# A state-space layer and a feed-forward layer, forward and backward, on one core: factored convolution transforms, smaller feed-forward chunks, and parameter gradients made where their operands are

## The chip, the cores and the metric

One core of one Trainium2 chip. The metric is the time on the device of one execution, in microseconds. Most executions of a kernel agree within 0.3%. One run of the kernel before, at 4296 us in one of the series, was slow and is in no ratio.

In the profile's lines PE is the matmul engine and PEld its loads of stationary operands; DVE (vector), ACT (activations) and POOL (GpSimd) do the elementwise work; SP issues transfers (DMA). Matmuls leave their sums in banks of PSUM (tiles named ps), and to evict a sum is to copy it out with DVE or ACT.

## The reference, cut to what matters

```
xn  = layernorm(x)                                  # x: 2048 x 576, bf16
K   = Re( sum_n C * exp(dt*A*l) * dt*B )            # S4 kernel: 576 channels, 128 states, 2048 lags
y   = irfft(rfft(pad(xn)) * rfft(pad(K))) + xn*Dskip
ffn = (relu(xn @ W_gate) * (xn @ W_up)) @ W_down    # 576 -> 4608 -> 576
out = x + y + ffn
# returned: out and, for the given grad_out, the gradients of x, A, B, C (re, im), log_dt, Dskip, W_gate, W_up, W_down
```

Two independent parts (S4 and FFN) share a core. FFN is mostly matmul. S4 is mostly vector work: 128 x 2048 complex exponentials for each of 576 channels, and the reductions of their gradients, between four rounds of Fourier transforms.

## The kernel before: the parts that matter

Two Python generators give out FFN and S4 work in small units. S4 gets 0.8 units of estimated time for each of FFN's. When FFN has run out, the rest of S4 runs alone, and then the final tiles, which add the two parts' results and finish the gradient of x.

```
# pacing
while True:
    r = next(fgen, None)
    if r is None: break
    ffn_t += float(r)
    while not s4_done and s4_t < ratio * (ffn_t - lead):     # ratio = 0.8, lead = 40
        c = next(sgen, None)
        ...
for _ in sgen: pass
final_main(...)

# kernel rows (gen_kgen): Y is made, used for K, and also stored for the gradients
nc.vector.tensor_tensor(Yr[:], E[:], c_[:], op=ALU.mult)
nc.vector.tensor_tensor(Yi[:], E[:], s_[:], op=ALU.mult)
...
nc.sync.dma_start(y_dram[0, :, ...], Yr[:]);  nc.sync.dma_start(y_dram[1, :, ...], Yi[:])

# transforms (gen_fwd): dense 1024-column DFT matrices, KC = 4 accumulated matmuls a tile (8 and more in the inverse)
for kc in range(KC):
    nc.tensor.matmul(ps[:, :DH], lhsT=Fmat[:, kc, mc*P:(mc+1)*P], rhs=sig[:, kc, hf*DH:(hf+1)*DH], ...)

# end of the S4 gradients (gen_grads), five times
ft = ctx.enter_context(tc.tile_pool(name="g_ft", bufs=2))
...
ob = ft.tile([P, N], BF16, name="g_ob")
nc.scalar.activation(ob[:dsz], src[:dsz], ACT.Copy, scale=dtk)
nc.sync.dma_start(outs[name][d0:d0 + dsz, :], ob[:dsz])                     # six of these
...
nc.sync.dma_start(outs["log_dt"][d0:d0+dsz].rearrange("(p o) -> p o", o=1), dldb[:dsz])  # 128 values, one a partition
```

Of the kernel before, what the change touches and what calls it, by code (L numbers as in the profile page):

```python
# [9 lines left out]
BF16 = mybir.dt.bfloat16  # L10
# [7 lines left out]
Q = 128  # L18
# [3 lines left out]
CFG = dict(mode="interleave", ratio=0.8, lead=40.0, ffn_prio="none")  # L22
STATE = dict(phase="none")


def dchunks(D):
    return [(k, k * P, min(P, D - k * P)) for k in range((D + P - 1) // P)]


def padded(D):  # L30
    return ((D + P - 1) // P) * P


def make_consts(nc, consts, NA):
    C = {}
    C["ident_bf"] = consts.tile([P, P], BF16, name="ident_bf")
    make_identity(nc, C["ident_bf"][:])
    C["ident_f"] = consts.tile([P, P], F32, name="ident_f")
    make_identity(nc, C["ident_f"][:])
    for name, val in (("mcol", MAGIC), ("hpcol", math.pi / 2), ("nhpcol", -math.pi / 2)):  # L40
        C[name] = consts.tile([P, 1], F32, name=name)
        nc.vector.memset(C[name][:], val)
    C["bvals"] = consts.tile([P, Q], F32, name="bvals")
    nc.gpsimd.iota(C["bvals"][:], pattern=[[1, Q]], base=0, channel_multiplier=0, allow_small_or_imprecise_dtypes=True)
    C["lvals"] = consts.tile([P, NA], F32, name="lvals")
    C["qavals"] = consts.tile([P, NA], F32, name="qavals")
    nc.gpsimd.iota(C["qavals"][:], pattern=[[Q, NA]], base=0, channel_multiplier=0, allow_small_or_imprecise_dtypes=True)
    nc.gpsimd.iota(C["lvals"][:], pattern=[[P, NA]], base=0, channel_multiplier=1, allow_small_or_imprecise_dtypes=True)
    pcol = consts.tile([P, 1], F32, name="pcol")
    nc.gpsimd.iota(pcol[:], pattern=[[0, 1]], base=0, channel_multiplier=1, allow_small_or_imprecise_dtypes=True)  # L50
    half = consts.tile([P, 1], F32, name="halfp")
    nc.vector.tensor_scalar(half[:], pcol[:], 0.5, -0.25, op0=ALU.mult, op1=ALU.add)
    nc.vector.tensor_scalar(half[:], half[:], MAGIC, None, op0=ALU.add)
    nc.vector.tensor_scalar(half[:], half[:], MAGIC, None, op0=ALU.subtract)
    par = consts.tile([P, 1], F32, name="par")
    nc.vector.scalar_tensor_tensor(par[:], half[:], -2.0, pcol[:], op0=ALU.mult, op1=ALU.add)
    C["sgn"] = consts.tile([P, 1], F32, name="sgn")
    nc.vector.tensor_scalar(C["sgn"][:], par[:], -2.0, 1.0, op0=ALU.mult, op1=ALU.add)
    C["nsgn"] = consts.tile([P, 1], F32, name="nsgn")
    nc.vector.tensor_scalar(C["nsgn"][:], par[:], 2.0, -1.0, op0=ALU.mult, op1=ALU.add)  # L60
    return C


def transpose_blocks(nc, psum_t, src, nblk, ident_bf):
    pt = psum_t.tile([P, 8, P], BF16, name="pt")
    for k in range(nblk):
        nc.tensor.transpose(out=pt[:, k, :], in_=src[:, k * P:(k + 1) * P], identity=ident_bf[:])
    return pt


def ln_forward(tc, nc, ctx, x_ap, g_ap, L, D, xn_dram, rinv_all, xnT_dram, gT_dram, psum_t, ident_bf):
    ST = L // P
    DP = padded(D); NDK = DP // P
    big = ctx.enter_context(tc.tile_pool(name="ln_big", bufs=1))
    sb = ctx.enter_context(tc.tile_pool(name="ln_sb", bufs=3))
    tb = ctx.enter_context(tc.tile_pool(name="ln_tb", bufs=2))
    small = ctx.enter_context(tc.tile_pool(name="ln_small", bufs=1))
    nsub = 2 if D > nc.vector.BN_STATS_FMAX else 1
    assert D % nsub == 0
    fsz = D // nsub  # L80
    x_all = big.tile([P, ST, D], BF16, name="x_all")
    nc.sync.dma_start(x_all[:], x_ap.rearrange("(t p) d -> p t d", p=P))
    mv_all = small.tile([P, ST, nc.vector.BN_AGGR_DIM], F32, name="mv_all")
    for st in range(ST):
        stats = sb.tile([P, nsub, nc.vector.BN_STATS_DIM], F32, name="stats")
        for s in range(nsub):
            nc.vector.bn_stats(out=stats[:, s, :], in_=x_all[:, st, s * fsz:(s + 1) * fsz])
        nc.vector.bn_aggr(out=mv_all[:, st, :], in_=stats[:])
    mvb = small.tile([P, ST, 2], BF16, name="mvb")
    nc.vector.tensor_copy(mvb[:], mv_all[:])  # L90
    mvf = small.tile([P, ST, 2], F32, name="mvf")
    nc.vector.tensor_copy(mvf[:], mvb[:])
    veb = small.tile([P, ST], BF16, name="veb")
    nc.vector.tensor_scalar(veb[:], mvf[:, :, 1], 1e-5, None, op0=ALU.add)
    sdb = small.tile([P, ST], BF16, name="sdb")
    nc.scalar.activation(sdb[:], veb[:], ACT.Sqrt)
    sdf = small.tile([P, ST], F32, name="sdf")
    nc.vector.tensor_copy(sdf[:], sdb[:])
    nc.vector.reciprocal(rinv_all[:], sdf[:])
    GRP = 4 if ST % 4 == 0 else 1  # L100
    for st0 in range(0, ST, GRP):
        xT_st = tb.tile([P, NDK, GRP * P], BF16, name="xT_st")
        gT_st = tb.tile([P, NDK, GRP * P], BF16, name="gT_st")
        for j in range(GRP):
            st = st0 + j
            xc = sb.tile([P, D], BF16, name="xc")
            nc.vector.tensor_scalar(xc[:], x_all[:, st, :], mvf[:, st, 0:1], None, op0=ALU.subtract)
            xn = sb.tile([P, DP], BF16, name="xn")
            if DP > D:
                nc.gpsimd.memset(xn[:, D:DP], 0.0)  # L110
            nc.vector.tensor_scalar(xn[:, 0:D], xc[:], rinv_all[:, st:st + 1], None, op0=ALU.mult)
            nc.sync.dma_start(xn_dram[st * P:(st + 1) * P, :], xn[:, 0:D])
            pt = transpose_blocks(nc, psum_t, xn, NDK, ident_bf)
            nc.scalar.copy(xT_st[:, :, j * P:(j + 1) * P], pt[:, 0:NDK, :])
            gt = sb.tile([P, DP], BF16, name="gt")
            if DP > D:
                nc.gpsimd.memset(gt[:, D:DP], 0.0)
            nc.gpsimd.dma_start(gt[:, 0:D], g_ap[st * P:(st + 1) * P, :])
            pt2 = transpose_blocks(nc, psum_t, gt, NDK, ident_bf)
            nc.vector.tensor_copy(gT_st[:, :, j * P:(j + 1) * P], pt2[:, 0:NDK, :])  # L120
        nc.sync.dma_start(xnT_dram[:, :, st0 * P:(st0 + GRP) * P], xT_st[:])
        nc.gpsimd.dma_start(gT_dram[:, :, st0 * P:(st0 + GRP) * P], gT_st[:])


def load_dn(nc, pool, ap, D, N, name, eng):
    DK = dchunks(D); NDK = len(DK)
    t = pool.tile([P, NDK, N], BF16, name=name)
    nfull = sum(1 for (_, _, dsz) in DK if dsz == P)
    if nfull > 0:
        eng.dma_start(t[:, 0:nfull, :], ap[0:nfull * P, :].rearrange("(k p) n -> p k n", p=P))  # L130
    for (k, d0, dsz) in DK:
        if dsz < P:
            eng.dma_start(t[:dsz, k, :], ap[d0:d0 + dsz, :])
    return t


def load_dt(nc, pool, log_dt, D, name):
    DK = dchunks(D); NDK = len(DK)
    ldt = pool.tile([P, NDK], BF16, name=name + "_l")
    nc.vector.memset(ldt[:], 0.0)  # L140
    for (k, d0, dsz) in DK:
        nc.sync.dma_start(ldt[:dsz, k:k + 1], log_dt[d0:d0 + dsz].rearrange("(p o) -> p o", o=1))
    dt = pool.tile([P, NDK], F32, name=name)
    nc.scalar.activation(dt[:], ldt[:], ACT.Exp)
    return dt


def s4_params(tc, nc, ctx, D, N, aps, ident_f, psum_s4, T_dram):
    assert N == P
    DK = dchunks(D)  # L150
    pool = ctx.enter_context(tc.tile_pool(name="s4p", bufs=1))
    tmp = ctx.enter_context(tc.tile_pool(name="s4p_tmp", bufs=2))
    raw = {name: load_dn(nc, pool, aps[name], D, N, f"raw_{name}", nc.sync) for name in ("A_re", "A_im", "B_re", "B_im", "C_re", "C_im")}
    dt = load_dt(nc, pool, aps["log_dt"], D, "dt")
    dt2pi = pool.tile([P, len(DK)], F32, name="dt2pi")
    nc.vector.tensor_scalar(dt2pi[:], dt[:], 1.0 / TWO_PI, None, op0=ALU.mult)
    for (k, d0, dsz) in DK:
        ar = tmp.tile([P, N], F32, name="ar")
        nc.vector.tensor_scalar(ar[:dsz], raw["A_re"][:dsz, k, :], dt[:dsz, k:k + 1], None, op0=ALU.mult)
# [20 lines left out]
def gen_kgen(tc, nc, ctx, L, D, N, T_dram, xp_dram, y_dram, k_dram, C, psum_s4, SC=32, DG=8):  # L180
# [12 lines left out]
    mcol, hpcol, bvals = C["mcol"], C["hpcol"], C["bvals"]  # L193
    qav = C["qavals"]
    k_view = k_dram[:].rearrange("(a p) d -> p a d", p=P)
    LAG = 1
    pending = []
    kst_done = []
    kst_count = {}
# [864 lines left out]
```

## Time and profile before

| before | value |
|---|---|
| time, median of 5 | 2557.6 us (2547.6 to 2564.5) |
| mean granted clock | 0.90 |
| PE at its streaming rate (worked out in the prediction: 1869; from the trace's matmuls: 1858) | 73% of the span |

The page's engine shares, its slices (each digit a fortieth of the span, in tenths) and its chain by engine:

```profile
PE 2048.3 (80%) x15768; PEld 1270.0 (50%) x15768; DVE 1762.9 (69%) x4152; ACT 1427.4 (56%) x2431; POOL 508.0 (20%) x782
...
PE   3899999887997999995499998989998999755400
...
DVE  6798999998999532222999998981220228899944
ACT  2789898988988755531253353354372345445421
...
PEclk8899999998998999998699999999999999756655
...
PE 26%; DVE 21%; issue 17%; ACT 16%; DMA 15%; POOL 3%; SPq 1%; POOLq 0%; ACTq 0%; DVEq 0%
```

Read the slices as columns. PE is at 9 where DVE is at 2 (the transforms). PE's last six digits fall from 7 to 0 while DVE is at 8 and 9, and at 4 in the last two. The chain is spread over everything, a fourth of it PE. Nothing is saturated from end to end.

### The profile page before, as it was taken

The numbers are of one execution on the slowest core, as the hardware profiler recorded it, in microseconds if no ns is written. First come the engines' busy times: TensorE is split into PE (matmuls) and PEld (weight loads), VectorE is DVE, ScalarE is ACT, GpSimd is POOL, SyncE is SP. The second block draws the span as 40 slices with busy tenths as digits, with TensorE's granted clock in tenths as the row PEclk, the third lists the DMA queues.
The fourth block names the chain that finished last, engine by engine and source line by source line (L and its number), as shares of the span: only waits on it lengthen the run. The fifth ranks groups of instructions, "written<-read, shape, count | busy, mean of one in ns | idle before, by whom it ended". The sixth has DMA issues, their size and how long they took to land.

```text
span 2555.4 us, 43178 instructions
## 1 busy us (share of the span) xinstructions
PE 2048.3 (80%) x15768; PEld 1270.0 (50%) x15768; DVE 1762.9 (69%) x4152; ACT 1427.4 (56%) x2431; POOL 508.0 (20%) x782
## 2 busy tenths in 40 slices
PE   3899999887997999995499998989998999755400
PEld 2464554554465466652254454455565665555300
DVE  6798999998999532222999998981220228899944
ACT  2789898988988755531253353354372345445421
POOL 2111121111022111110142233132011112222310
PEclk8899999998998999998699999999999999756655
DMA  7446558556666655466266657457445658776563
GB/s 223 143 143 196 139 127 210 143 126 152 175 146 150 168 139 143 136 176 161 63 162 154 165 114 189 114 114 168 97 105 162 169 148 220 220 215 193 158 146 90
DMA packets 481526, 393.59 MB, mean 154 GB/s; under 512 B 271232, under 2 KB 430496, under 8 KB 478240
## 3 DMA queue, kind: packets, MB, share of 16 engines
q1 hardware_dynamic: 424288, 287.60, 39.9%
q0 software_dynamic: 57024, 103.23, 19.4%
q8 instruction: 123, 2.02, 0.3%
q14 instruction: 91, 0.75, 0.1%
HBM read 229.46 MB, written 161.25 MB: 153 GB/s over the span
## 4 chain that ended last, share of the span: by engine, by line
PE 26%; DVE 21%; issue 17%; ACT 16%; DMA 15%; POOL 3%; SPq 1%; POOLq 0%; ACTq 0%; DVEq 0%
PE ps_s L351 4%; DMA out_dram<-g_ob 3%; PE ps_s L449 3%; PE ps_mm L754 3%; PE ps_mm L752 3%; PE pt L771 2%; PE ps_mm L750 2%; ACT y_E L240 2%; PE ps_mm L785 2%; PE ps_mm L780 2%; PE ps_mm L787 2%; ACT y_c L272 1%; ACT y_s L269 1%; DMA f_gtt<-gT_dram 1%; DMA ffn_acc<-so 1%
## 5 line engine op out<-in xcount | busy, mean ns | idle before, releaser
L762 DVE SCALAR_TENSOR_TENSOR upm<-ps_mm,upb 128x512 bf16<-128x512 f32 x144 | 98.5, 684 | 289.0 <-ACT upb L758 289.0
L820 PE MATMUL ps_mm<-dgN,xs 128*128 128x512 bf16 x720 | 270.3, 383 | 14.2 <-ACT dWdT_sb L822 7.1
L821 PE MATMUL ps_mm<-duN,xs 128*128 128x512 bf16 x720 | 268.6, 383 | 3.4 <-ACT dWdT_sb L822 2.0
L819 PE MATMUL ps_mm<-hN,gs 128*128 128x512 bf16 x720 | 257.8, 382 | 8.9 <-DMA gs<-in_grad_out_dram 8.9
L752 PE MATMUL ps_mm<-xT,wu 128*128 128x512 bf16 x720 | 205.6, 393 | 37.2 <-ACT upb L758 37.2
L796 POOL DMA_DIRECT2D ffn_acc<-so x128 | 118.2, 923 | 492.0 <-ACT so L781 419.3
L750 PE MATMUL ps_mm<-xT,wg 128*128 128x512 bf16 x720 | 201.9, 384 | 8.7 <-DMA wg<-in_B_W_gate_dram 8.7
L785 PE MATMUL ps_mm<-wgT,dgT 128*128 128x288 bf16 x1152 | 196.6, 286 | 8.3 <-ACT so L781 4.5
L754 PE MATMUL ps_mm<-gTt,wdT 128*128 128x512 bf16 x720 | 199.6, 394 | 0.0
L787 PE MATMUL ps_mm<-wuT,duT 128*128 128x288 bf16 x1152 | 190.9, 286 | 0.0
L780 PE MATMUL ps_mm<-wd,hT 128*128 128x288 bf16 x1152 | 175.4, 287 | 9.7 <-ACT so L781 8.4
L781 ACT CAST so<-ps_mm 128x288 bf16<-128x288 f32 x288 | 109.1, 404 | 98.9 <-PE ps_mm L780 47.2
L797 POOL DMA_DIRECT2D dxf_acc<-sx x128 | 116.9, 914 | 106.9 <-DVE sx L791 72.5
L780 PEld LDWEIGHTS <-hT 128*128 128x128 bf16 x1152 | 111.4, 98 | 44.6 <-issue 12.0
L476 PE MATMUL ps_s<-ident_bf,YA 128*128 128x128 bf16 x1152 | 117.9, 275 | 19.4 <-DMA YA<-y_dram 9.6
L785 PEld LDWEIGHTS <-dgT 128*128 128x128 bf16 x1152 | 111.9, 98 | 37.5 <-issue 10.4
L822 ACT CAST dWdT_sb<-ps_mm 128x512 bf16<-128x512 f32 x45 | 26.3, 585 | 181.8 <-PE ps_mm L819 181.8
L787 PEld LDWEIGHTS <-duT 128*128 128x128 bf16 x1152 | 112.1, 98 | 27.4
L476 PEld LDWEIGHTS <-YA 128*128 128x128 bf16 x1152 | 102.5, 127 | 34.5 <-issue 16.1
L820 PEld LDWEIGHTS <-xs 128*128 128x128 bf16 x720 | 70.5, 98 | 97.0 <-issue 11.7
L449 PE MATMUL ps_s<-Wl,Gmat 128*128 128x288 bf16 x768 | 111.7, 290 | 8.5 <-ACT dK_sb L669 3.8
L791 DVE CAST sx<-ps_mm 128x288 bf16<-128x288 f32 x176 | 78.1, 451 | 55.9 <-PE ps_mm L787 45.7
(336 smaller groups left out, 4980.7 us busy)
## 6 DMA issues: line engine op xcount, KB each, us to landing
YA<-y_dram SPq DMA_DIRECT2D x72, 512.0 KB, 4.3
xT<-xnT_dram SPq DMA_DIRECT2D x36, 640.0 KB, 4.6
gTt<-gT_dram SPq DMA_DIRECT2D x36, 640.0 KB, 6.2
ffn_acc<-so POOLq DMA_DIRECT2D x144, 144.0 KB, 4.0
dxf_acc<-sx POOLq DMA_DIRECT2D x144, 144.0 KB, 3.8
gs<-in_grad_out_dram SPq DMA_DIRECT2D x72, 256.0 KB, 3.5
xs<-xn_dram SPq DMA_DIRECT2D x72, 256.0 KB, 3.8
y_dram<-y_Yi SPq DMA_DIRECT2D x72, 256.0 KB, 2.8
```

The lines of the kernel that those rows point to most:

```text
L449: nc.tensor.matmul(ps[:, :DH], lhsT=lt, rhs=rh, start=(i == 0), stop=(i == len(mms) - 1))
L476: nc.tensor.transpose(out=psb[:, dl * N:(dl + 1) * N], in_=ya[:, h0 + dl, :], identity=C["ident_bf"][:])
L750: nc.tensor.matmul(ps_g[:, :SGW], lhsT=wg[:, k, ft * P:(ft + 1) * P], rhs=xT[:, k, :], start=(k == 0), stop=(k == NDK - 1))
L752: nc.tensor.matmul(ps_u[:, :SGW], lhsT=wu[:, k, ft * P:(ft + 1) * P], rhs=xT[:, k, :], start=(k == 0), stop=(k == NDK - 1))
L754: nc.tensor.matmul(ps_h[:, :SGW], lhsT=wdT[:, k, ft * P:(ft + 1) * P], rhs=gTt[:, k, :], start=(k == 0), stop=(k == NDK - 1))
L780: nc.tensor.matmul(ps_o[:, :DH], lhsT=hT[:, ft, j * P:(j + 1) * P], rhs=wd[:, ft, hf * DH:(hf + 1) * DH], start=(ft == 0), stop=(ft == FTC ...
L785: nc.tensor.matmul(ps_x[:, :DH], lhsT=dgT[:, ft, j * P:(j + 1) * P], rhs=wgT[:, ft, hf * DH:(hf + 1) * DH], start=(ft == 0), stop=False)
L787: nc.tensor.matmul(ps_x[:, :DH], lhsT=duT[:, ft, j * P:(j + 1) * P], rhs=wuT[:, ft, hf * DH:(hf + 1) * DH], start=False, stop=(ft == FTC - 1))
L796: nc.gpsimd.dma_start(ffn_acc[st * P:(st + 1) * P, :], so[:], accum_op=ALU.add)
L819: nc.tensor.matmul(ps_d[:, :Fc], lhsT=gs[:, sl, :], rhs=hN[:, st, :], start=(st == 0), stop=(st == ST - 1))
L820: nc.tensor.matmul(ps_g[:, :Fc], lhsT=xs[:, sl, :], rhs=dgN[:, st, :], start=(st == 0), stop=(st == ST - 1))
L821: nc.tensor.matmul(ps_u[:, :Fc], lhsT=xs[:, sl, :], rhs=duN[:, st, :], start=(st == 0), stop=(st == ST - 1))
```

## The change

The mathematics stays and nearly every line is new. Its intent: less PE work, none of S4 left over when FFN ends, and vector work spread evenly. At its core (cuts marked):

```
-    nc.tensor.matmul(... lhsT=Fmat[:, kc, ...] ...)            # x4 a tile, dense 1024-column matrices
+    # 2048 = 128 x 16: 128-point factor, 16-point factor, product, and back
+    nc.tensor.matmul(ps[:, :DH], lhsT=self.S1[:, n2, ri, :], rhs=halves(n2, hf), start=True, stop=True)
+    nc.tensor.matmul(ps[:, :DH], lhsT=CC[:], rhs=src[:, o, hs], ...); nc.tensor.matmul(ps[:, :DH], lhsT=sm[:], ...)
...
-    nc.sync.dma_start(y_dram[0, ...], Yr[:])                   # reloaded in a gradient phase of its own
+    self.group(pend.pop(0), ytp, gp)                           # K and the gradient products from Y while it is there
...
-Fc=512  (9 chunks), xT single-buffered
+Fc = 384 (12 chunks), xT, gT, gq, xs double-buffered; output tiles put between the gate tiles
...
+class Balance:                                                 # each eviction goes to the less loaded of DVE and ACT
+    def copy(self, out, in_, cols, scale=None, fp32=True): ...
...
-while not s4_done and s4_t < ratio * (ffn_t - lead):           # ratio = 0.8
+while s4_open and stt < PACE * (ft - start):                   # PACE = 0.86
...
+    for i in range(4):                                         # final tiles within the last weight gradients
+        self.dw_down(c, i)
+        for t in range(i * 2, i * 2 + 2): final(t)
...
-    nc.sync.dma_start(outs["log_dt"][...].rearrange("(p o) -> p o", o=1), dldb[:dsz])
+    nc.sync.dma_start(self.outs["log_dt"][...].rearrange("(o p) -> o p", o=1), dldb[0:1, 0:dsz])   # one row
```

Down weights have one buffer, `self.wd`. In program order `load_w(c)`, which fills it for chunk c, stands before the four last output tiles of chunk c-1:

```
self.load_w(c)                               # overwrites wd
for j in range(JS):
    self.outdx(c - 1, NSG - 1, j)            # reads wd: now the next chunk's
```

## The prediction

> **What bounds the kernel now.** I read the page's engine shares and its 40 slices first, then busy time per stage (stretches cut where the program changes phase), then the chain of waits in the last 150 us, then the groups by shape, for durations. No engine is busy all the time: PE 80%, DVE 69%, ACT 56%. The stretches show why.
>
> ```profile
> core 0: us, PE busy (x) PEld busy (x) DVE busy (x) ACT busy (x) POOL busy (x), PEclk, DMA share, GB/s
> 0.00:72.00 72.00, 21.63 (x172) 16.46 (x172) 41.81 (x162) 16.53 (x30) 19.87 (x67) 0.80 0.76 233
> ...
> 128.00:768.00 640.00, 577.39 (x4538) 341.39 (x4537) 595.20 (x995) 570.03 (x793) 110.79 (x140) 0.96 0.61 155
> 896.00:1152.00 256.00, 248.21 (x1731) 155.33 (x1729) 68.72 (x178) 127.90 (x287) 35.31 (x47) 0.99 0.56 150
> 1152.00:1216.00 64.00, 32.32 (x160) 14.53 (x159) 17.26 (x67) 7.00 (x12) 7.33 (x14) 0.80 0.66 158
> 1216.00:1728.00 512.00, 437.65 (x2875) 253.32 (x2875) 476.11 (x1186) 220.28 (x445) 147.18 (x223) 0.94 0.56 135
> 1728.00:2048.00 320.00, 297.71 (x2079) 191.41 (x2077) 52.46 (x120) 134.22 (x231) 52.87 (x76) 0.98 0.56 139
> ...
> 2206.00:2410.00 204.00, 116.30 (x1616) 104.02 (x1615) 203.87 (x670) 101.71 (x191) 50.58 (x85) 0.62 0.69 203
> 2410.00:2555.00 145.00, 8.16 (x20) 3.22 (x20) 71.81 (x262) 34.33 (x88) 22.26 (x39) 0.50 0.49 117
> ```
>
> The columns after the engines are granted clock, DMA share and GB/s. The feed-forward part (FFN) runs beside the state-space part (S4), whose phases follow one another. Making the convolution kernel (128 to 768) loads DVE to 93% and ACT to 89%. The forward transforms (896 to 1152) and the inverse ones (1728 to 2048) are PE's, with DVE at 27% and 16%. The products (1216 to 1728) are DVE's, at 93%, with ACT at 43%. At 1152 the Dskip gradient waits for single-buffered loads and PE falls to half. From 2206 FFN has run out: 204 us of parameter gradients bound by DVE, then 145 us in which nearly nothing runs. In the first 72 us there is only layer norm. So the imbalance in time is the bound, more than any engine's total.
>
> The chain inside the last 145 us:
>
> ```profile
> by line: DMA out_dram<-g_ob 60.6%; issue 4.2%; ACT g_ob L551 3.3%; DMA hN<-dxf_acc 3.2%; DMA Rk<-r_dram 2.5%; DMA out_dram<-hN 2.4%; PE ps_s L544 2.3%; ACT hN L876 1.0%; ACT gd_dcr L546 0.9%; ACT L144 0.9%; ACT hN L884 0.8%; SPq L872 0.6%;
> ```
>
> 61% of that stretch is the landing of small gradient tiles whose buffer is wanted again: pure latency.
>
> How densely PE can stream is read from starts in the timeline, because the ends overlap:
>
> ```profile
> 2012.68 1.03 PE L752 MATMUL ps_mm<-xT,wu 128*128 128x512 bf16 x4
> 2013.54 1.24 PE L754 MATMUL ps_mm<-gTt,wdT 128*128 128x512 bf16 x5
> 2014.62 0.78 PE L780 MATMUL ps_mm<-wd,hT 128*128 128x288 bf16 x5
> ...
> 2018.58 1.14 PE L780 MATMUL ps_mm<-wd,hT 128*128 128x288 bf16 x8
> 2019.56 0.65 PE L785 MATMUL ps_mm<-wgT,dgT 128*128 128x288 bf16 x4
> ```
>
> Five of 512 columns take 2014.62 - 2013.54 = 1.08 us, 0.216 each; eight of 288 take 0.98 us, 0.1225 each.
>
> **What the Trainium skill says.** "TensorE: Matmul & The Clock Gate", section "Wait — 56ns, not 53.3ns?": a warm start-to-start is N/2.4 GHz plus about 2.5 ns, with a floor near 25 ns. The trace agrees (0.216 and 0.1225 us), so I estimate 62.5 ns for 144 columns, 162.5 for 384, 55.5 for 128, 29 for 64 and 26 for 16 and 32. The same page, "Part 1: The HAM clock gate", says an idle PE drops to half clock: the tail's 0.62 and 0.50 agree. "ScalarE: Activation LUTs", "What ACT_TABLE_LOAD costs", gives 1283 ns a load; the trace has exactly that, and 100 loads in its six main rows. "VectorE: DVE Perf Modes", "The perf-mode tier table", says two-tensor ops run double rate in bf16 and single in fp32 or from PSUM; agreed, 422 ns against 683 at 512 columns.
>
> ```profile
> L764 DVE TENSOR_TENSOR dgT<-dhb,upm 128x512 bf16<-128x512 bf16 x144 | 60.8, 422 | 28.4 <-ACT dhb L760 26.3
> L254 DVE TENSOR_TENSOR x_Xr<-x_e,x_c 128x512 bf16<-128x512 f32 x18 | 12.3, 683 | 0.1
> L240 ACT ACT_TABLE_LOAD x33 | 42.3, 1283 | 0.6
> L781 ACT CAST so<-ps_mm 128x288 bf16<-128x288 f32 x288 | 109.1, 404 | 98.9 <-PE ps_mm L780 47.2
> ```
>
> **The change, part by part.** It is a rewrite of the same mathematics, so I count instructions of the built programs and price them from the rows.
>
> PE before: 4320 x 0.216 = 933; 5344 of 288 (3456 FFN, 1888 transforms) x 0.1225 = 655; some 3760 transposes x 0.0555 = 209; 2304 small x 0.026 = 60; fp32 and rest 12: about 1869 us at full clock, 73% of the span. PE after: FFN up and gate 2160 x 0.216 = 467; output side 3456 x 0.1225 = 423; weight gradients, no longer padded to 640 rows, 2304 x 0.0625 + 1536 x 0.1625 + 1152 x 0.029 = 144 + 250 + 33; 3616 transposes = 201; the convolution as 128- and 16-point factors instead of dense 1024-column matrices, 1152 x 0.1225 = 141; small 60, rest 12: about 1731. PE saves 138 us.
>
> DVE after, raw row sums: FFN masks and products 144 x (684 + 427 + 422 + 416) = 281; evictions 436, 201; kernel rows Y 144 x (683 x 3 + 421 + 2 x 422) = 477; gradient products and reductions 576 x about 420 = 243; X 155; spectral products, now one pass per frequency, 122; base and final tiles 129; norm, twiddles, parameters 121: about 1730. Neighbours overlap by about 0.08 us (an operation of 1.22 us starts 1.13 before the next), some 250 us over 3570 instructions: about 1480 net against 1763. ACT after: 902 + 192 evictions of 288 x 0.404 to 0.410 = 443; 505 bf16 copies 310; other evictions 320; FFN Relu and copy 172; sines and exponentials 365; 40 table loads instead of over 100, 51: about 1660, net some 1480 against 1427. It takes evictions from DVE by a running balance.
>
> Twelve column chunks of 384 replace nine of 512: 192 more output evictions of 288 and more reloads, the price of room for double-buffered inputs.
>
> Schedule: layer norm by groups of four tiles, so PE starts FFN at about 25 us, not 72. S4 is paced by 0.86 of FFN's estimated time; in PE's order its last matmul stands at about 37 fortieths of the work, so the 350 us tail goes. Parameter gradients are made next to their kernel rows (no reload of 36.9 MB, no separate phase), and final tiles sit within the last weight-gradient matmuls.
>
> Sum by stage. Head 25; FFN before S4, 90 of PE at 0.85, 106. Transforms first half 210 at 0.9, 233. Kernel and gradients: PE 1089; vector work 1510 (S4) + 819 (FFN beside it) raw, less some 283 overlap, over two engines 1023 each. The stage 128 to 768 of before kept PE streaming at about 0.84 with DVE 0.93 and ACT 0.89, so PE at 0.87 to 0.89 looks reachable at 0.83: 1240. Second half of the transforms 266 at 0.9, 296. FFN alone 110 at 0.92, 120. Behind it some 40 us, where the final tiles (16 x 4.2 us of DVE) outlast 37 us of matmul. Together 2060; with a little for waits at the joints, 2070.
>
> **Rivals.** First, three engines near 85% in order may stall each other. For it: the kernel's output side now fills a PSUM bank in 0.37 or 0.73 us, before 0.49 or 0.98, and must be evicted through the same four banks, while ACT runs 1.0 to 1.3 us operations; S4 has two banks. At 0.78 of streaming it is 1731 / 0.78 + 60 = 2280 us. Against it: in the old stage with both vector engines near 90%, PE still streamed 0.84. Second, vector work bounds the middle: if strided evictions cost as the old Kst copy did (771 ns for 128 elements; 144 x 0.5 = 72 us more) and half of the overlap, 150 us, is not had, each vector engine has 1023 + 111 = 1134 there, and at 0.87 that is 1300 instead of 1240: 2130. Third, the mixing works better, PE at 0.91 throughout: 1731 / 0.91 + 60 = 1960. Fourth, transfers: acc reads and writes grow with twelve chunks, but Y no longer goes through memory, so I estimate 360 MB against 394; hidden.
>
> **Range and chances.** 2070 us, 1960 to 2190 for 8 in 10. A gain of 2% needs under 2506; the tail alone is 350 us, so even with the first rival it holds: faster 0.96, same 0.02, slower 0.02.
>
> **What would show it.** Right: granted clock above 0.94 until the last slices; PE's first FFN matmul before 35 us; DVE near 1480 and ACT near 1480 busy, both even over the span; DVE share in the transforms well over the old 16 to 27%; under 80 us after the last output matmul. Wrong: waits of PE for evictions (ps_mm, ps_s released by ACT or DVE) of several hundred us; a middle where PE streams under 0.8; S4 still running after FFN.

## The result, and the profile after

The order of the load of `wd` shown above is a defect of the changed kernel, not of the kernel before. The changed kernel, with which the defect came, took **2112.0 us** (2103.6 to 2115.1, 8 runs) against 2558.8 (2547.6 to 2568.0, 15 runs): ratio **0.825**, 95% interval 0.8233 to 0.8267. Ratios here are the mean time of one kernel's fast runs over the mean of the other's in the same rounds, so not quite the ratio of the quoted medians.

The same parts of the page, after:

```profile
PE 1914.3 (91%) x17726; PEld 1314.0 (62%) x17726; DVE 1527.7 (72%) x3550; ACT 1456.4 (69%) x3070; POOL 227.9 (11%) x292
...
PE   7989999879899999999899999899899899978796
...
DVE  8544665499877898759989599886885375646594
ACT  5655664489778889659889589877786456732563
...
PEclk9999999989999999999999999999999999989899
...
PE 43%; ACT 18%; DMA 11%; DVE 9%; issue 8%; SPq 0%; POOL 0%; ACTq 0%; DVEq 0%; POOLq 0%
```

No digit of PE is below 6, the granted clock never leaves 8 to 9, and PE's share of the chain went from 26 to 43%. By stage (columns: stretch, length, then busy time and instructions of PE, its weight loads, DVE, ACT, POOL; then clock, DMA share, GB/s). The rows are transforms up to the first kernel row; kernel rows and parameter gradients; the other transforms; FFN alone; and the time behind FFN's last output matmul:

```profile
100.00:424.00 324.00, 292.70 (x2305) 192.43 (x2305) 175.60 (x394) 188.57 (x448) 28.73 (x47) 0.98 0.79 236
424.00:1616.00 1192.00, 1109.99 (x11382) 782.61 (x11381) 989.74 (x2292) 964.81 (x1935) 126.65 (x135) 0.97 0.50 112
1616.00:1980.00 364.00, 323.46 (x2505) 212.24 (x2505) 209.48 (x466) 179.81 (x435) 21.48 (x25) 0.94 0.82 243
1980.00:2060.00 80.00, 70.42 (x518) 46.89 (x517) 60.55 (x142) 49.71 (x111) 12.92 (x15) 0.96 0.98 283
2060.00:2114.00 54.00, 37.35 (x412) 27.97 (x409) 25.96 (x55) 16.32 (x33) 0.86 (x1) 0.93 0.81 245
```

DVE and ACT are at 83 and 81% in the middle, and now at 54 to 58% and 49 to 58% in the transforms, where DVE had 16 to 27%.

**Where the time came from** (442 us between the two traced runs). Busy PE is not PE at its peak, so I count for every matmul of the trace its columns at the start-to-start time of its shape (0.216 us for 512 columns, 0.1225 for 288, and so on, as in the prediction) and set the sum against the length of the stretch.

| stretch | before: length, streamed, lost | after: length, streamed, lost |
|---|---|---|
| head | 128, 58, 70 | 100, 68, 32 |
| body | 2078, 1733, 345 (83% streamed) | 1960, 1617, 343 (83% streamed) |
| tail | 349, 67, 283 | 53, 35, 18 |
| whole | 2555, 1858, 697 | 2113, 1720, 393 |

(Head: up to 128 and to 100 us. Tail: from 2206 on, where FFN ran out, and from 2060 on.) By this count the body streams as well as it did before, no better. One rate in it is too low for the changed kernel: its 32-column gradient matmuls started 57 ns apart, not 26 (experiment 7), which is some 32 us more PE time, all in the body (84% then). The gain is 138 us of PE work (some 106 with that correction) and 304 us (some 336) of time without it, most of it head (38) and tail (265). What was to be explained is therefore how the tail could go.

### The profile page after: what moved, and what is told of

Read it like the earlier page. It is cut to its first block, busy times and chain, and to the rows that moved or that the text cites.

```text
span 2113.3 us, 45588 instructions
## 1 busy us (share of the span) xinstructions
PE 1914.3 (91%) x17726; PEld 1314.0 (62%) x17726; DVE 1527.7 (72%) x3550; ACT 1456.4 (69%) x3070; POOL 227.9 (11%) x292
## 3 DMA queue, kind: packets, MB, share of 16 engines
q10 hardware_dynamic: 2112, 2.36, 0.4%
## 4 chain that ended last, share of the span: by engine, by line
PE 43%; ACT 18%; DMA 11%; DVE 9%; issue 8%; SPq 0%; POOL 0%; ACTq 0%; DVEq 0%; POOLq 0%
PE ps_mm L279 11%; PE ps_mm L235 10%; PE ps_mm L313 6%; PE ps_s L523 3%; PE ps_s L755 3%; PE ps_mm L299 2%; PE pt L261 2%; ACT YT L64 2%; DMA wd<-in_B_W_down_dram 2%; PE ps_s L524 2%; ACT osx L64 2%; PE ps_s L748 2%; ACT ysn L714 1%; DMA gq<-gq_dram 1%; ACT ycs L716 1%
## 5 line engine op out<-in xcount | busy, mean ns | idle before, releaser
L64 ACT CAST osx<-ps_mm 128x288 bf16<-128x288 f32 x656 | 249.9, 413 | 102.1 <-PE ps_mm L279 100.6
L284 POOL DMA_DIRECT2D acc_dram<-osx x176 | 151.8, 863 | 1331.8 <-ACT osx L64 932.3
L235 PE MATMUL ps_mm<-gT,wdT 128*128 128x512 bf16 x720 | 190.4, 382 | 2.5 <-DVE upm L244 2.5
L299 PE MATMUL ps_mm<-gq,hN 128*128 128x144 bf16 x2304 | 170.0, 231 | 21.9 <-DMA gq<-gq_dram 21.7
L299 PEld LDWEIGHTS <-hN 128*128 128x128 bf16 x2304 | 157.9, 101 | 30.6 <-DMA gq<-gq_dram 17.7
L759 DVE TENSOR_TENSOR pr<-X,ps_s 128x256 f32<-128x256 f32 x288 | 108.2, 416 | 68.2 <-PE ps_s L755 66.1
L313 PE MATMUL ps_mm<-dgN,xs 128*128 128x384 bf16 x768 | 144.7, 328 | 6.5 <-DMA xs<-xs_dram 6.5
L313 PE MATMUL ps_mm<-duN,xs 128*128 128x384 bf16 x768 | 138.3, 326 | 1.0 <-ACT upb L242 1.0
L64 ACT COPY YT<-ps_s 128x1024 bf16<-128x1024 bf16 x105 | 107.6, 1025 | 5.8 <-PE ps_s L748 3.8
L242 ACT CAST upb<-ps_mm 128x512 bf16<-128x512 f32 x144 | 85.4, 593 | 35.4 <-PE ps_mm L235 30.9
```

The costliest lines, as they stand in the source:

```text
L64: self.nc.scalar.copy(out, in_)
L235: nc.tensor.matmul(ps[:], lhsT=w[:, k, fs], rhs=rhs[:, k, :], start=(k == 0), stop=(k == NK - 1))
L242: nc.scalar.copy(upb[:], ps_u[:])
L284: nc.gpsimd.dma_start(g.acc_dram[:, t, :, :], o[:], accum_op=ALU.add)
L299: nc.tensor.matmul(ps[:, (ft - f) * 144:(ft - f + 1) * 144], lhsT=self.hN[:, st, ft * P:(ft + 1) * P], rhs=gq[:, st, :], start=(st == 0), ...
L313: nc.tensor.matmul(ps[:, :Fc], lhsT=xs[:, st, :], rhs=src[:, st, :], start=(st == 0), stop=(st == ST - 1))
```

## The experiments

**1. No interleaving, in either kernel.** One theory (A): interleaving FFN and S4 is what carries the time, and a better overlap is where the gain is. The rival (B): most of it is less work. `PACE = 0.0` in the changed kernel makes FFN run first and S4 after it; `mode="serial"` in the kernel before makes S4 run first.

```
-PACE = 0.86
+PACE = 0.0                                   # serial
-CFG = dict(mode="interleave", ...
+CFG = dict(mode="serial", ...                # b_serial
```

> The changed kernel with the pace at 0, so the state-space part runs behind the feed-forward part. Theory A (the gain is mostly that the state-space work lies beside FFN from start to end): FFN alone about 1455 us of PE at 0.92 is 1580, then the state-space part alone, bound by DVE in its middle (about 900) and by latency in its transforms (about 300), then the end: 2750 to 2900 us, slower than the kernel before. Rival B (the gain is mostly less work): little depends on the interleave, under 2300 us.

> The kernel before with its own serial mode, the state-space part first and FFN behind it; to be held beside the changed kernel's serial run, where FFN alone ended at 1607 us and the state-space part took 1470 us. Theory A1 (FFN itself became denser: double-buffered inputs, output tiles between the gate tiles): FFN alone takes 1720 to 1850 us here. Theory A2 (only the interleaving changed): FFN alone takes 1607 plus some 40 us for its padding. The state-space part alone: its DVE and ACT work is larger, 1500 to 1700 us.

Measured: changed kernel 3080.1 us (3078.4 to 3081.7; ratio to before 1.200), kernel before 3561.9 (3555.0 to 3568.8; ratio 1.388). First the changed kernel, FFN and then S4 with the final tiles; below it the kernel before, S4, FFN, final tiles:

```profile
0.00:1607.00 1607.00, 1517.88 (x13055) 1042.66 (x13198) 633.66 (x1504) 654.73 (x1345) 200.35 (x269) 0.99 0.60 147
1607.00:3082.00 1475.00, 571.86 (x4528) 339.71 (x4528) 1080.31 (x2415) 740.67 (x1355) 20.44 (x24) 0.53 0.27 83
```

```profile
0.00:1860.00 1860.00, 513.15 (x5544) 397.77 (x5544) 1275.73 (x2912) 894.00 (x1237) 212.19 (x383) 0.60 0.36 111
1860.00:3446.00 1586.00, 1537.11 (x10079) 883.90 (x10214) 573.08 (x1301) 507.93 (x990) 267.97 (x353) 0.99 0.49 102
3446.00:3554.00 108.00, 1.05 (x15) 0.71 (x12) 63.71 (x132) 25.90 (x49) 25.00 (x47) 0.52 0.72 226
```

S4 alone, with the final tiles, takes 1475 us now. Before, it took 1860 + 108, of which some 65 are the layer norm that the other order counts with FFN (its last tile was done at 62 us, the S4 parameters follow): about 1903. So S4 became some 430 us shorter by itself. FFN alone, with the layer norm, hardly moved: 1586 + 65 = 1651, now 1607. That is Theory A2 (1607 and some 40 for the padding): FFN itself did not become denser. Cut by phase, the two traces show where S4 shortened: transforms, products and the Dskip sum from 792 us (660 to 1452) to 514 (1607 to 1821 and 2690 to 2990; a part of the new ones ran before 1607), kernel rows and parameter gradients from 1003 to 869, final tiles from 108 to 87.

Interleaving hides 3080 - 2112 = 968 us now and hid 3562 - 2569 = 993 before. So the two parts in a row became 482 us shorter and 25 us less of them is hidden: that is the whole gain of 457. Both serial times lie above what was expected. Of the first two theories, A has the size of the overlap, nearly a thousand microseconds in either kernel, but it did not get better; B has where the gain is. S4 alone, final tiles included, was 250 us longer than the FFN it should lie beside and is now 130 us shorter. That this is why there is no tail is argued from here and from experiment 2; no run puts a long S4 into the changed kernel, and the parts of the rewrite were not tried one by one.

**2. The old kernel's tail, by pace alone.**

```
-ratio=0.8
+ratio=1.1                                    # b_ratio
```

> The kernel before with its pace ratio at 1.1 instead of 0.8, nothing else: by the order of PE's instructions the parameter gradients then lie beside FFN and FFN ends last. Theory A (schedule): most of the 350 us tail goes, 2250 to 2350 us. Rival B (work): the DVE-bound stages only stretch, because DVE (1763 us) and ACT are as busy as before; 2450 to 2550. My own guess is 2350, the rest of the way to 2112 being less work and the even spread inside the phases.

Measured 2632.4 us (2625.8 to 2634.3): ratio 1.0247 (1.0225 to 1.0269), slower, outside both theories, where I had expected a gain of 8%. The stage of kernel rows and the stretch in which FFN is left over:

```profile
256.00:768.00 512.00, 370.20 (x2981) 221.22 (x3016) 483.01 (x765) 455.28 (x600) 76.63 (x87) 0.85 0.55 141
...
2176.00:2560.00 384.00, 269.08 (x1786) 152.33 (x1806) 162.07 (x485) 115.30 (x249) 65.92 (x96) 0.86 0.56 111
```

The parameter gradients did move beside FFN, and behind PE's last matmul (2517) only 107 us, of final tiles, were left. But in the first stretch, with DVE and ACT at 94 and 89% as before, S4 gets on no faster, and less FFN is allotted to it: PE streamed 323 of 512 us (63%, where the old stage had 0.84). The FFN that was saved up ran at the end, streaming 244 of 341 us. At this ratio, the only other one run, pace moved the shortage and did not remove it.

**3. The old kernel's tail, by its buffers.** The prediction read 61% of the last 145 us as small gradient tiles whose buffer is wanted again. So give the pool six buffers instead of two:

```
-ft = ctx.enter_context(tc.tile_pool(name="g_ft", bufs=2))
+ft = ctx.enter_context(tc.tile_pool(name="g_ft", bufs=6))    # b_tail
```

> The kernel before with six buffers instead of two for the small tiles of the last gradient phase, where 61% of the last 145 us were landings of g_ob. If that latency is the tail's bound: minus 60 to 90 us, ratio 0.965 to 0.977. If something else stands behind it (the queue that issues, the final tiles): minus 20 or less.

Measured 2567.0 us (2557.1 to 2575.3): ratio 1.0003 (0.9983 to 1.0023). Nothing. The transfers of the last 146 us say why (bytes of one, and median us from issue to landing), kernel before and then this run:

```profile
out_dram<-g_ob SPq DMA_DIRECT2D x24, 32.0 KB, 3.5
...
out_dram<-dldb SPq DMA_DIRECT2D x4, 0.2 KB, 16.3
```

```profile
out_dram<-g_ob SPq DMA_DIRECT2D x24, 32.0 KB, 16.8
...
out_dram<-dldb SPq DMA_DIRECT2D x4, 0.2 KB, 18.5
```

The smallest transfer is the slowest: 128 two-byte values of the log_dt gradient, written from one partition each, take 16 us, and what is issued behind it lands late. (To read 128 such values into the partitions, `g_dt_l`, took 3.3 us in the same stretch.) In the kernel before, a 32 KB tile issued 0.47 us after one of them held ACT for 14.7 us, until its buffer came free:

```profile
2446.23 0.38 SPq L587 DMA_DIRECT2D out_dram<-dldb  x1
...
2446.70 0.38 SPq L552 DMA_DIRECT2D out_dram<-g_ob  x1
...
2463.02 0.40 ACT L551 ACTIVATE g_ob<-u,g_dt 128x128 bf16<-128x128 f32 x1 [14.70 <-DMA out_dram<-g_ob]
```

The median hides two kinds: 8 of the 30 tiles of that stretch were issued within 3.5 us behind such a write and took 15.1 to 16.2 us, landing just after it; the other 22 took at most 6.3. Four waits of ACT of this kind (13.0 to 15.2 us) make 58 of the 145 us. With more buffers the tiles are issued sooner and land later, 16.8 us instead of 3.5. So the wait that had been put down to the buffer seems to have been for the transfer ahead in the queue. I did not run the kernel before with that write made as one row, as the changed kernel makes it, so this is the likely cause of those waits and not a shown one; shown is that it isn't the number of buffers.

**4. What the transforms and the transfers cost in the changed kernel.** `dbl` does all 1152 matmuls of the transforms twice (141 us more of PE streaming). `noacc` writes the FFN sums plainly instead of adding to memory. Its output is wrong, which doesn't matter for the time.

```
+for _ in range(2):                            # dbl, around each transform matmul
     nc.tensor.matmul(ps[:, :DH], lhsT=self.S1[:, n2, ri, :], rhs=halves(n2, hf), start=True, stop=True)
-nc.gpsimd.dma_start(g.acc_dram[:, t, :, :], o[:], accum_op=ALU.add)
+nc.gpsimd.dma_start(g.acc_dram[:, t, :, :], o[:])            # noacc
```

> The changed kernel with every matmul of the transforms (1152 of 288 columns) done twice, results unchanged: 141 us of PE streaming added in the stages where PE streamed at 0.81 and 0.78 instead of the 0.9 that I had assumed. If PE is the bound there: plus 130 to 150 us, about 2250. If transfers or evictions are the bound there and PE has room: plus 70 or less, 2115 to 2180.

> The changed kernel with plain writes in place of the accumulating ones for the FFN output (wrong first two outputs on purpose): less reading of memory and cheaper packets, at equal issue counts. If transfers bound the transform stages and the end (DMA share 0.80 to 0.92 there): minus 30 to 80 us. If they are hidden: within 10 us of 2112.

Measured: dbl 2215.4 us (ratio 0.8624, 0.8604 to 0.8644), so 96 (by the ratios) to 103 us (by the medians) of the 141 arrive, between the two expectations: the transform stages are mostly, not wholly, PE's. noacc 2076.0 (0.809, 0.8069 to 0.8111): 36 to 41 us less, spread over middle and end, at the low end of what was expected if transfers bound. So what the adding costs, in the largest kind of transfer here, is mostly hidden, not wholly.

**5. The defect corrected.**

```
+    def load_wd(self, c): ...                 # the load of wd, taken out of load_w
     for j in range(JS):
         self.outdx(c - 1, NSG - 1, j)
+    self.load_wd(c)                           # wdfix
```

> The changed kernel with the load of the down weights moved behind the last output group of the chunk before. (In the changed kernel that group waits for, and multiplies with, the next chunk's weights: an error in the first output, too small for the comparison to see.) PE waited 20.7 us for this load in 8 waits. If the waits lie on the path: minus 15 to 25 us, 2085 to 2100. If the slack elsewhere takes them up, or the transposes of the new weights now wait instead: within 8 us.

Measured 2082.4 us (2075.7 to 2087.9): ratio 0.8112 (0.8085 to 0.8139), 1.7% (30 to 35 us) less than the changed kernel, a little more than expected, and right. The wrong order had also cost a wait, the second here, which is no longer among the longest in wdfix (waits of PE in the changed kernel: what waited, for what; us in total, times, longest):

```profile
PE ps_mm L299 <- DMA gq<-gq_dram: 21.7, 12, 7.7
PE ps_mm L279 <- DMA wd<-in_B_W_down_dram: 20.7, 8, 4.3
```

**6. PSUM banks,** the prediction's first rival, on wdfix: FFN 3 banks instead of 4, S4 3 instead of 2.

```
-g.psum_mm = pool("psum_mm", 4, ...)    g.psum_s4 = pool("psum_s4", 2, ...)
+g.psum_mm = pool("psum_mm", 3, ...)    g.psum_s4 = pool("psum_s4", 3, ...)     # wd_ps3
```

> On top of wdfix: the feed-forward output side and weight gradients have 3 PSUM banks instead of 4, the S4 part 3 instead of 2. First rival of the prediction (output banks, evicted late, stall PE in order): slower than wdfix by over 2% (ratio above 0.827), with waits of PE for evictions of ps_mm grown by 50 us or more. Rival B (S4's two banks make the transforms stream at 0.81 instead of 0.9): faster, the first transform stage 20 to 40 us shorter and the time 1 to 2% below wdfix (ratio 0.795 to 0.803). Theory A (neither count of banks binds): within 1% of wdfix (0.803 to 0.819).

Measured 2087.8 us: ratio 0.8117 (0.8101 to 0.8133), the same as wdfix. The first transforms did get shorter (the first kernel row came at 406 us instead of 422), but no denser: PE streamed 218 of 276 us there, against 240 of 293, because less FFN lay beside them, and the rest gave it back. So this trade of banks gains nothing; as both counts moved at once, it does not say what either is worth alone.

**7. The middle: three ways to lighten PE.** Unexpected in the trace was that the 32-column matmuls of the gradients, whose moving operand takes a value every 64 bytes, start every 57 ns; the old ones of the same size, packed, did so every 26. Summed over all 1152 that is 63 us against 31, some 32 us of PE, all in the middle. `dkc` (on the changed kernel) has GpSimd write the operand packed. `wd_dkv` (on wdfix) has ACT and DVE do it. `wd_flat` (on wdfix, wrong) reads 32 neighbouring values of the operand as it lies and adds no instruction.

```
-rhs=dkc[:, :, :, dd + dl]                                     # [P, 2, 16, 32]: stride 64 bytes
+dkr = gp.tile([P, ST, SC], BF16, name="pr"); dma(dkr, ...)    # dkc, wd_dkv
+E1.copy(dkc[:, :, 0, :].rearrange("p d a -> p a d"), dkr)     # dkc: GpSimd; wd_dkv: ACT
+E2.tensor_tensor(dkc[:, :, 1, :]..., dkr, lv, mult)           # dkc: GpSimd; wd_dkv: DVE
+rhs=dkc[:, dd + dl, :, :]
+rhs=dkc.flat[(dd + dl)*32 : (dd + dl)*32 + 32]                # wd_flat
```

> The changed kernel with the small gradient operand laid out so that a matmul's 32 moving columns are adjacent instead of 64 bytes apart; GpSimd does the rearranging, 18 more copies. In the changed kernel these 1152 matmuls start 57 ns apart, before 26 ns: 1152 x 0.031 = 36 us of PE. If the spacing comes from the stride: back to about 26 ns; and if PE bounds the middle (it streamed 0.84 there): minus 15 to 35 us. If the vector engines bound the middle: spacing falls, time stays within 8 us.

> On top of wdfix (ratio 0.811 to before): the kernel gradient rows are laid out contiguously again, but the 18 copies are made by ACT and the 18 multiplications by DVE, and GpSimd does no arithmetic. In dkc the 32-column matmuls started every 25 ns instead of 57 (28 us of PE saved), but DVE operations that ran beside GpSimd's 36 copies and multiplications (2.7 to 3.2 us each, 106 us in all) took about 50 us longer than the same operations elsewhere. Theory A (GpSimd's arithmetic held DVE up, and this ate the gain): faster than wdfix by 10 to 25 us, ratio 0.802 to 0.807. Rival B (the middle is bound by the vector engines' work and its dependencies, a lighter PE gives nothing there; ACT and DVE have some 20 us more): same as wdfix or slower, ratio 0.810 to 0.816.

> On top of wdfix (ratio 0.811 to before), wrong on purpose: the 32-column matmuls read 32 neighbouring values instead of 32 values 64 bytes apart, with no instruction added or moved and the same loads, so that only PE gets lighter, by 1152 times about 25 to 30 ns, some 28 us, all in the stage of kernel and gradients. Theory A (PE sets the pace of that stage): the whole gain arrives, 20 to 30 us less, ratio 0.800 to 0.804; then what dkc and wd_dkv lost was the price of their copies (a load that DVE and ACT wait for in order, GpSimd beside DVE). Rival B (the vector engines set the pace of that stage): nothing arrives, ratio 0.808 to 0.814, the stage as long as in wdfix and PE's waits in it grown by what it was relieved of.

| run | against | ratio to before | us gained or lost |
|---|---|---|---|
| dkc | changed kernel, 0.825 | 0.831 (0.8282 to 0.8338) | about +15 |
| wd_dkv | wdfix, 0.8112 | 0.8262 (0.8246 to 0.8277) | about +38 |
| wd_flat | wdfix, 0.8112 | 0.8053 (0.8028 to 0.8077) | about -15 |

(The last column is the difference of the two ratios times 2560.) In all three the matmuls start every 25 ns. What the packing cost instead, changed kernel, dkc, and wd_dkv:

```profile
L674 POOL TENSOR_TENSOR dkc<-dkc,lv 128x512 bf16<-128x512 bf16 x18 | 26.4, 1466 | 287.2 <-DMA dkc<-dk_dram 244.6 <-PE ps_s L783 15.3 <-PE ps_mm L279 11.4
L802 DVE TENSOR_TENSOR p<-Tt,raw 128x128 f32<-128x128 f32 x16 | 4.6, 287 | 11.0 <-ACT g_ob L794 11.0
```

```profile
L675 POOL COPY dkc<-pr 128x512 bf16<-128x512 bf16 x18 | 57.0, 3168 | 365.5 <-DMA pr<-dk_dram 326.4 <-PE ps_mm L235 34.4 <-PE ps_mm L279 4.7
L676 POOL TENSOR_TENSOR dkc<-pr,lv 128x512 bf16<-128x512 bf16 x18 | 48.8, 2709 | 0.0
L804 DVE TENSOR_TENSOR p<-Tt,raw 128x128 f32<-128x128 f32 x16 | 9.4, 590 | 10.9 <-ACT g_ob L796 10.5 <-ACT Tt L786 0.2
```

```profile
L681 ACT COPY dkc<-pr 128x512 bf16<-128x512 bf16 x18 | 43.7, 2426 | 17.1 <-DMA pr<-dk_dram 17.0
L682 DVE TENSOR_TENSOR dkc<-pr,lv 128x512 bf16<-128x512 bf16 x18 | 43.1, 2393 | 20.3 <-DMA pr<-dk_dram 20.1
```

In dkc, GpSimd's 106 us of arithmetic stretched the DVE operations beside it: the same multiplication (L802, now L804) takes 590 instead of 287 ns on average. Taking every DVE operation that overlaps one of GpSimd's 36 and comparing it with the median of its own line elsewhere gives 50 us of excess, against 5 in the changed kernel. The Trainium skill has this: "SBUF — State Buffer", section "SBUF: two separate sides", says that DVE and GpSimd share one port pair, held as an exclusive lock for a whole instruction. The trace agrees, and six DVE operations of dkc that had one of their two inputs in PSUM (`upm`, 512 columns) took 686 ns beside GpSimd as elsewhere.

wd_dkv has no GpSimd arithmetic, and lost more. Writing 512 two-byte values 64 bytes apart took 2.4 us on ACT and on DVE alike, where I had reckoned with some 20 us for all 36 together, and both engines stood about 1 us each time for the load. That put 43 us of work and 17 to 20 us of waiting on each of the two engines at 80% and more. The waiting is not a price of the packing itself: the load was issued a median 3.9 us before its use and took 3.8, into buffers (`pr`) that the gradient products use too. A load issued earlier, into a buffer of its own, was not tried, in dkc neither. "Advanced Engine Details and Errata", section "SBUF Cachelines", says that an access which goes to another 16-byte line each time is penalised; the trace agrees, and the page gives no size.

wd_flat, which has neither, gains some 15 of the 32 us: inside neither expectation (20 to 30, or nothing). In its trace the stage of kernel rows takes 1147 us instead of 1158. So in the middle a microsecond of PE is worth a third to a half, and vector work is dear: it looks as if PE and the vector engines bound it together.

**8. The middle, compressed.** I raised `PACE`, meaning to stretch S4. I had the knob the wrong way round: S4 may be PACE times as far as FFN, so 0.98 makes S4 faster.

```
-PACE = 0.86
+PACE = 0.98                                  # wd_p98, on wdfix
```

> On top of wdfix: S4 is paced by 0.98 of the FFN's estimated time instead of 0.86, so the stage of kernel and gradients is stretched and the inverse transforms come nearer to the end. Theory A (in the middle the vector engines' load keeps PE at 0.84; spread over more FFN it streams better): middle stage longer, but its PE streaming 0.86 or more, and the time 0 to 1.5% below wdfix (ratio 0.799 to 0.811) if S4 still ends before FFN. Rival B (S4 now ends at or after FFN, and its latency lies bare at the end): slower by 1 to 3% (0.819 to 0.835), more than 80 us after the last FFN output matmul.

Measured 2126.6 us (2125.7 to 2129.7): ratio 0.8274 (0.8259 to 0.8288), slower than wdfix by 42 us. The last kernel row came at 1494 us instead of 1580, as it must. The stage in wdfix, then here:

```profile
384.00:1584.00 1200.00, 1120.07 (x11458) 788.88 (x11552) 1009.87 (x2328) 978.05 (x1965) 126.12 (x142) 0.98 0.51 116
```

```profile
384.00:1500.00 1116.00, 1005.79 (x10307) 707.96 (x10390) 967.91 (x2241) 919.62 (x1832) 113.68 (x124) 0.95 0.48 109
```

DVE goes from 84 to 87%, and PE streamed 880 of 1116 us, 79% instead of 84%. That answers to Theory A's reason (vector load in the middle holds PE down), run in the other direction; the expectation's numbers, written for the misread knob, don't apply. Rival B named the right size for another cause: the last transform matmul came at 1832 us, long before FFN's last output matmul (2073), with 55 us behind that. Whether a lower pace than 0.86 gains was not run.

**The best right version is wdfix: 2082.4 us,** ratio 0.811. wd_flat is faster but wrong.

## Why the prediction was right, point by point

Predicted 2070 (1960 to 2190), measured 2112.

- **PE's work**: 1731 predicted, 1720 from the trace at the same rates. Right, but for one rate: the 32-column gradient matmuls, priced at 26 ns, started 57 ns apart, some 32 us more.
- **Vector work**: DVE and ACT near 1480; measured 1528 and 1456. The raw sums (1730 and 1660) measured 1746 and 1688. Right within 3%; the overlap of neighbours was 218 us for DVE, less than the 250 reckoned.
- **The middle**: 1240 us; measured 1188 (424 to 1612), with DVE at 0.83 as reckoned and PE streaming 0.845, where 1089 / 1240 is 0.88; with the 57 ns counted it is 0.88. So the reading from the old stage of 128 to 768 held. The size came out shorter because less FFN lay there: 1008 us of PE instead of 1089.
- **The term that was mis-sized**: "Transforms first half 210 at 0.9, 233" and "Second half of the transforms 266 at 0.9, 296". Measured 288 (136 to 424) and 368 (1612 to 1980), 127 us more, with PE streaming 237 at 0.82 and 285 at 0.77. More FFN work lay there (46 us of PE), and the 0.9 was a guess from the old transforms, whose accumulations (4 matmuls forward, 8 or more in the inverse) left 288 sums to evict, where the new ones leave 672. Middle (-52), and FFN alone with the end (133 instead of 160), paid most of it back; with the start of S4 at 136 instead of 131 it makes the 42 to 53 us. That errors of 127 and 79 us nearly cancelled is luck, and so is part of the closeness of the sum.
- **What the 0.8 consists of stays open in part.** dbl shows PE to be the larger part of it, wd_ps3 that a third S4 bank taken from FFN makes it no denser, noacc that the adding in the transfers is a small part. PE's named waits in the first transform stretch (up to 384 us) are each under 5 us in total.
- **Table loads**: 40 as counted, 51 us.
- **First rival** (stalls on banks, 2280): no. PE's named waits for ACT and DVE, of all kinds, sum to 104 us, not several hundred, and wd_ps3 changes the time by nothing. **Second rival** (vector engines bound the middle, 2130): its mechanism is there, as wd_dkv, wd_flat and wd_p98 show, but its sizes weren't: the new strided evictions took 231 ns for 64 elements, 33 us in all, not 72 us more. **Third** (0.91 throughout): no, 0.83. **Fourth** (transfers hidden, 360 MB): 358.7 MB; what noacc took away was worth some 40 us, so "hidden" was off by that much.
- **The tail**: "pure latency" of buffers was the wrong reading of a right number (experiment 3). That it would go was right. The reason in the prediction, imbalance in time, needs what experiments 1 and 2 add: S4 became shorter by itself, and pacing alone made things worse.
- **Signs**: clock 0.968, and 0.93 or more in every stretch; first FFN matmul at 17.9 us (predicted under 35); 54 us behind the last output matmul (under 80). All as said. That the transforms' share of DVE would rise held too (54 to 58%), though even over the span it is not, with 83% in the middle.
- **Not seen**: the order of the load of `wd`. It lay open in the program, and cost 30 us and the correctness of 512 rows.

## What to carry to other kernels

When two parts are interleaved, time each alone: if one is longer than its cover, shorten it; pacing, in both kernels, only moved the shortage to another stage. Count streaming by stage as columns times the rate of their shape: here the body stayed at 83 to 84% through a complete rewrite, and the gain was in less work and in head and tail. And before packing an operand for PE, price the packing on the engine that does it: two-byte scatter and GpSimd beside DVE cost more than the some 30 us they were to save.

## What the Trainium skill lacked or had wrong

- "TensorE: Matmul & The Clock Gate", section "Wait — 56ns, not 53.3ns?": the start-to-start of N columns has no term for how the moving operand lies. 32 bf16 columns 64 bytes apart started every 57 ns, 32 packed ones every 25 to 26.
- "Advanced Engine Details and Errata", section "SBUF Cachelines": names a penalty for a new line at each access, without a size, and no page gives one for two-byte values written by DVE or ACT. 512 of them written 64 bytes apart took 2393 ns on DVE and 2426 on ACT; GpSimd took 3168 for the copy and 2709 for the multiplication, against 1466 packed, beside DVE work, so not for the layout alone.
- "SBUF — State Buffer", section "SBUF: two separate sides": right about the shared port pair; the section gives no size for arithmetic on both engines. 106 us of GpSimd arithmetic cost DVE about 50 us beside it, a 287 ns operation averaging 590.
- "DMA: Bandwidth & Descriptors": no duration for a write of single two-byte values to memory. 128 of them, one from each partition, took 16.3 us to land, where reading 128 into the partitions took 3.3 and most 32 KB tiles at most 6.3.
